# The opening of a planned convolution and max-out kernel: VectorE's tap products read the softmax weights from a PSUM bank, TensorE sums the taps of four tiles, and the opening's list is written anew

## The chip, the cores and the metric

The kernel runs on one core of one Trainium2 chip. The time is device microseconds (us) of one execution of the whole program. The kernel before takes 1434.37 us, the median of three runs (1434.16 to 1434.89).

The core has five engines that run side by side, each through its own list of instructions in order: TensorE (PE in the profile; its weight loads are PEld), VectorE (DVE), ScalarE (ACT), GpSimd (POOL) and SyncE (SP), which here issues the DMAs. SBUF is the working memory; PSUM has eight banks, which TensorE writes.

## The reference, cut to what matters

```python
w = softmax(weight_gen, over the 7 taps)          # [8, 4160, 8 heads, 7 taps]
out = einsum('bshk,bskhg->bshg', w, x_unf)        # x_unf: each token with the 6 before it
x = out.reshape(33280, 192)
h = maximum(maximum(x @ w1, x @ w2), x @ w3)      # 192 -> 768
return h @ w_out                                  # 768 -> 192
```

Everything is fp32. The weights come as float64 (the kernel reads them as pairs of 32-bit words).

## The kernel before

**Tiling.** 33280 tokens are 260 tiles of 128, and 65 chunks of 4 tiles. Chunk 0 is a load of its own; from chunk 1 on two chunks share one load of tokens (tile `xt`, two buffers) and of tap weights (`wt`).

**A chunk's way.** The softmax of the tap weights runs over DVE, POOL and ACT (lines 366 to 405). For each tile a *tap product* (L428) multiplies the tokens with the weights, 7 taps by 192 numbers, into a buffer `r`, and a *sum* on DVE (L440) adds the 7 taps into `acc`. The product runs on POOL, or on DVE for the tiles in `TAPS_ON_VECTOR`. Then the tile is turned, so that features lie on partitions: for chunks 0 and 1 by TensorE (L481, L482) into two PSUM banks, for the others by DVE and 24 ACT moves into `room`. ACT and DVE or POOL split the result into a high and a low part (`xa_hi`, `xa_lo`, `xb`, `xc`).

**The maxima.** max(xw1, xw2, xw3) is taken as xw1 + max(0, x(w2-w1), x(w3-w1)). So `up` multiplies with two differences (high and low parts `wa_hi`, `wa_lo`, `wb_hi`, `wb_lo`) for each of the six blocks j of 128 hidden features, ACT and DVE take the maximum, and split it into `h_hi` and `h_lo`. `down` multiplies those with w_out, and x with `wca` and `wcb`, the product of w1 and w_out, which the opening makes (`compose`, L870). Both have their matmuls at line 922. Each is cut into two half-height rows of 64 partitions, planned as two streams, L and U, that TensorE runs at the same time.

**What sets the order.** Nothing is written in program order. The kernel makes tasks with an engine, an assumed cost, dependencies, a due time and the buffers they hold; `Plan.order` (line 71) plays them through event by event and lets each free engine take the ready task with the earliest due. Two kinds, the TensorE streams L and U, run in the order in which they are added. For chunks 0 and 1 that order is the hand-written list `OPENING` (line 222): loads, softmax, `singles` (float64 words to fp32, lines 638 to 689), `a` and `b` (the differences, on POOL, or on TensorE where `MODE` says L), `turn` (w1 turned for `compose`, L851 and L853), `turn x` (a tile turned), `parts`, `up`, `compose`, `down`. Tables beside it say which engine takes what: `MODE`, `CLAMP_ON_POOL`, `ON_POOL_FIRST`, `LOAD_DUE`, `TAPS_ON_VECTOR`, `SUMS_ON_TENSOR` (empty before).

An engine's own list is then fixed: an instruction that waits holds up all behind it on that engine.

```python
        ("a", 2): ("POOL", "DVE"),     # line 186: difference on POOL, its low part ("rest") on DVE
        ("b", 2): ("L", "DVE"),        # line 189: difference on TensorE, rest on DVE
    SUMS_ON_TENSOR = ()
    TAPS_ON_VECTOR = ((0, 3), (1, 0), (1, 2))   # (chunk, tile)
```

Of the kernel before, what the change touches and what calls it, by code (L numbers as in the profile page):

```python
# [17 lines left out]
P = 128  # L18
# [21 lines left out]
class Plan:  # L40
# [13 lines left out]
    def add(self, engine, cost, emit, deps=(), due=None, holds=(), end=None):  # L54
# [6 lines left out]
        return t  # L61

    def start_by(self):

        for t in reversed(self.tasks):
            latest = [a.by - self.LATENCY - t.end for a in t.after]
            if t.due is not None:
                latest.append(t.due)
            t.by = min(latest, default=1e6)

    def order(self):
# [20 lines left out]
        def start(t, now):  # L92
# [53 lines left out]
def lightconv_maxout_kernel(  # L146
# [44 lines left out]
    CLAMP_ON_POOL = (("a", 1, 0), ("a", 1, 1), ("a", 2, 0), ("a", 2, 1), ("a", 2, 2), ("b", 1), ("d", 0), ("d", 1),)  # L191
    LOAD_DUE = {
        ("s", 0): -46,
        ("a", 0): -61,
        ("b",): -36,
        ("s", 1): -45,
        ("a", 1): -51,
        ("a", 2): -36,
        ("d",): -21,
    }  # L200
# [8 lines left out]
    for c in range(1, NC):  # L209
# [14 lines left out]
        ("load down",), ("softmax", 0), ("softmax", 1), ("singles", 0), ("singles", 1),  # L224
        ("singles", 2), ("singles down",), ("taps", 0), ("taps", 1), ("turn", 0), ("b", 2),
# [6 lines left out]
    )  # L232
# [67 lines left out]
    def vec(n):  # L300
        return 0.062 + 0.00104 * n
# [105 lines left out]

    parts_of, last_product = {}, {}

    def taps(c):  # L410
        s = super_of[c]
        la = (c - supers[s][0]) * TC
        hx, hw, ha = xts[s], wts[s], hold("acc")
        sums = []
        for t in range(TC):
            hr = hold("r")
            eng, cost = ("DVE", vec(D * K)) if (c, t) in TAPS_ON_VECTOR else ("POOL", 2.68)
            on = nc.vector if eng == "DVE" else nc.gpsimd
            by_tensor = (c, t) in SUMS_ON_TENSOR

            def product(t=t, hr=hr, on=on, by_tensor=by_tensor):
# [17 lines left out]
            def total(t=t, hr=hr):  # L439
                pin(nc.vector.tensor_reduce(buf(ha)[:, t], buf(hr), axis=AX.X, op=ALU.add))  # L440

            p = plan.add(
                eng, cost, product, [ready[s], *loads[s][1]], early(c, 3 * t - 17), [hr, hx, hw]
            )
            sums.append(
                (p, hr)
# [43 lines left out]
    def blocks(c, ha, sums):  # L490
# [19 lines left out]
        for q, f in enumerate(range(0, D, 32)):  # L510
            for p in range(0, P, 32):
# [6 lines left out]

                got.append(plan.add("ACT", 0.31, move, [turned], clock[0] - 2 + q, [hv]))
        return [hv], lambda: places()[:2], got  # L520

    def parts(c, hs, places, got):
# [13 lines left out]
            for h in halves  # L536
        ]
        name, cost = ("DVE", vec(CH)) if c < ON_TENSOR else ("POOL", gps(CH))
        eng = nc.vector if c < ON_TENSOR else nc.gpsimd
# [151 lines left out]
    w_hi, w_lo, b_hi, b_lo, one_a, one_b = {}, {}, {}, {}, {}, {}  # L691
    of_bank = {}

    def whole(cost, emit, deps, holds):

        got = plan.add(
            "L", cost, emit, [*deps, made, *u_last()], clock[0], holds, end=cost + 0.25
        )
        clock[0] += cost
        return got  # L700
# [22 lines left out]
    def difference(shape, w, of, deps, holds, on):  # L723
# [3 lines left out]
        if on == "POOL":  # L727
# [8 lines left out]
            )  # L736
            return w, d, holds
        hb = hold("bank")

        def mult():  # L740
# [13 lines left out]
        d = whole(0.1 + n * m * 0.0034, mult, [*deps, made_minus], [hb, *holds])  # L754
        return lambda: buf(hb)[:, : n * m].rearrange("p (i n) -> p i n", i=n), d, [hb]

    def rest(size, to, of, hi, deps, holds, on):

        eng = nc.gpsimd if on == "POOL" else nc.vector
        return plan.add(  # L760
# [4 lines left out]
    def differences_a(jp, first, last):  # L765
# [3 lines left out]
        n = last - first  # L769
        v, d, holds = difference(  # L770
            (n, 2 * P), lambda: buf(hx)[:, first:last],
# [8 lines left out]
        )  # L780
        lo = rest(
            2 * n * P, lambda: place_of(wa_lo), of, lambda: place_of(wa_hi).bitcast(F32), [hi],
            holds, then,
        )
        for i in range(first, last):
            w_hi[jp, i], w_lo[jp, i] = hi, lo

    def differences_b(jp):
        hq = hold("bhi")
        on, then = MODE["b", jp]  # L790
        v, d, holds = difference(
            (NI, P), lambda: b32[:, jp, 1:], lambda: b32[:, jp, 0], [one_b[jp]], [], on
# [3 lines left out]
        )  # L796
        b_lo[jp] = rest(
            2 * P, lambda: wb_lo[:, jp], v, lambda: buf(hq).bitcast(F32), [e], [*holds, hq], then
        )
        for odd, h in enumerate(halves):  # L800
# [285 lines left out]

    def ups(c, j):
        for i in range(NI):
            up(c, j, i)

    def singles_down():
# [6 lines left out]
        "turn x": turn_tokens, "parts": opening_parts,  # L1098
        "a": differences_a, "b": differences_b, "up": ups,
        "turn": turn_weights, "compose": compose, "down": downs,  # L1100
    }
# [54 lines left out]
```

## Time and profile before

| | |
|---|---|
| median of three runs | 1434.37 us |
| the profiled execution | 1434.17 us |
| its span, first to last instruction | 1432.4 us |
| so outside the span | 1.8 us |
| PE busy | 1399.5 us (98%) |
| ACT, POOL, DVE busy | 78%, 77%, 71% |
| mean granted TensorE clock | 0.993 |

The page's numbers are of one execution. PE is busy nearly all the time, but a matmul at half clock is as busy as one at full clock, so the share says little about the opening. What matters is read in stretches, and from the distance between the starts of neighbouring instructions.

### The profile page before, as it was taken

The page shows a single profiled execution, that of the slowest core. Times are in us where ns is not written, and L with a number is a line of the kernel's source. Part 1 is how long each engine was busy: PE and PEld are TensorE (multiplying, and loading weights), DVE is VectorE, ACT ScalarE, POOL GpSimd, SP SyncE. Part 2 cuts the span into 40 slices and gives each one's busy share as a digit, 9 for nine tenths or more (in the row PEclk, how much of TensorE's full clock was granted, in tenths as well). Part 3 has the DMA queues.
Part 4 walks back from the last instruction along what each step waited for, and adds up shares of the span by engine and source line. Part 5 has one row for each costly group of instructions (what it writes and reads, how often), then busy time and mean ns, then how long its engine had stood idle before and what let it go on. Part 6 is the DMA issues. An engine that isn't in the chain of part 4 may idle for free.

```text
span 1432.4 us, 37054 instructions
## 1 busy us (share of the span) xinstructions
PE 1399.5 (98%) x14884; PEld 1341.8 (94%) x14884; DVE 1021.9 (71%) x1394; ACT 1117.7 (78%) x2860; POOL 1105.1 (77%) x609
## 2 busy tenths in 40 slices
PE   3999999999999999999999999999999999999999
PEld 2799999999999999999999999999999999999998
DVE  8877777777677767767776776777687677767543
ACT  4378787888878878887887888888787887888773
POOL 6889978988686987868798786888868688886521
PEclk9799999999999999999999999999999999999999
DMA  7011111111111011111101111110111111110000
GB/s 251 1 57 69 68 57 69 68 65 61 68 69 57 33 60 57 68 68 68 58 23 69 58 68 68 57 66 26 63 63 69 68 57 42 50 58 24 24 23 24
DMA packets 23004, 85.09 MB, mean 59 GB/s; under 512 B 2488, under 2 KB 9144, under 8 KB 18864
## 3 DMA queue, kind: packets, MB, share of 16 engines
q1 hardware_dynamic: 22832, 82.73, 15.7%
q8 instruction: 116, 1.90, 0.5%
q14 instruction: 56, 0.46, 0.1%
HBM read 57.16 MB, written 25.56 MB: 58 GB/s over the span
## 4 chain that ended last, share of the span: by engine, by line
PE 77%; POOL 9%; DVE 8%; issue 3%; ACT 2%; DMA 0%; SPq 0%; DVEq 0%; POOLq 0%
PE bank L922 76%; POOL r L428 6%; DVE acc L440 3%; DVE bank L987 2%; DVE h_lo L998 1%; POOL h_lo L998 1%; POOL xb L549 1%; POOL xa_lo L544 1%; ACT h_hi L991 1%; DVE m L987 1%; ACT room L517 1%; ACT m L979 0%; POOL wt L403 0%; PE bank L870 0%; DVE r L428 0%
## 5 line engine op out<-in xcount | busy, mean ns | idle before, releaser
L428 POOL TENSOR_TENSOR r<-xt,wt 128x1344 f32<-128x1344 f32 x257 | 715.4, 2853 | 22.3 <-DMA xt<-in_x_dram 19.0
L922 PE MATMUL bank<-wo,h_hi 64*128 64x384 f32 x3120 | 660.1, 355 | 0.0
L922 PE MATMUL bank<-wo,h_lo 64*128 64x192 f32 x3120 | 593.5, 249 | 0.9
L922 PE MATMUL bank<-xa_hi,wa_hi 64*128 64x512 f32 x1560 | 507.9, 392 | 0.4 <-ACT wb_hi L805 0.3
L922 PE MATMUL bank<-xa_lo,wa_hi 64*128 64x512 f32 x1560 | 507.2, 391 | 0.0
L922 PE MATMUL bank<-xa_hi,wa_lo 64*128 64x512 f32 x1560 | 502.8, 388 | 0.0
L922 PEld LDWEIGHTS bank<-wo,h_lo 64*128 64x128 f32 x3120 | 482.5, 187 | 8.0 <-DVE h_lo L998 6.2
L517 ACT COPY room<-room 32x128 f32<-32x128 f32 x1512 | 447.9, 296 | 41.7 <-DVE room L506 19.3
L922 PEld LDWEIGHTS bank<-wo,h_hi 64*128 64x128 f32 x3120 | 475.3, 185 | 0.0
L440 DVE TENSOR_REDUCE acc<-r 128x192 f32<-128x1344 f32 x260 | 398.2, 1543 | 18.9 <-POOL r L428 18.5
L998 POOL TENSOR_TENSOR h_lo<-m,h_hi 128x512 fp32r<-128x512 f32 x132 | 174.2, 1320 | 179.9 <-ACT h_hi L991 179.7
L922 PE MATMUL bank<-xc,wb_hi 64*128 64x512 f32 x780 | 295.7, 388 | 0.0
L979 ACT ACTIVATE m<-bank 128x512 f32<-128x512 f32 x390 | 233.9, 600 | 64.8 <-PE bank L922 61.5
L922 PE MATMUL bank<-xb,wb_hi 64*128 64x512 f32 x780 | 280.4, 390 | 0.1
L922 PE MATMUL bank<-xc,wb_lo 64*128 64x512 f32 x780 | 276.5, 388 | 0.0
L922 PEld LDWEIGHTS bank<-xa_lo,wa_hi 64*128 64x128 f32 x1560 | 266.9, 185 | 9.2 <-POOL xa_lo L544 0.4
L922 PEld LDWEIGHTS bank<-xa_hi,wa_hi 64*128 64x128 f32 x1560 | 264.7, 185 | 10.5 <-ACT raw L858 0.8
L922 PEld LDWEIGHTS bank<-xa_hi,wa_lo 64*128 64x128 f32 x1560 | 265.1, 185 | 8.5
L987 DVE TENSOR_TENSOR bank<-bank,m 128x512 f32<-128x512 f32 x258 | 175.6, 694 | 81.7 <-PE bank L922 62.0
L1055 DVE TENSOR_TENSOR o<-bank,ob 128x192 f32<-128x192 f32 x260 | 90.2, 351 | 189.0 <-ACT ob L1048 188.5
L998 DVE TENSOR_TENSOR h_lo<-bank,h_hi 128x512 fp32r<-128x512 f32 x258 | 172.5, 680 | 51.2 <-ACT h_hi L991 49.9
L991 ACT CAST h_hi<-bank 128x512 fp32r<-128x512 f32 x258 | 151.1, 586 | 66.6 <-DVE bank L987 63.3
(92 smaller groups left out, 2046.1 us busy)
## 6 DMA issues: line engine op xcount, KB each, us to landing
xt<-in_x_dram SPq DMA_DIRECT2D x31, 1344.0 KB, 5.6
out_dram<-o SPq DMA_DIRECT2D x64, 384.0 KB, 2.3
wt<-in_weight_gen_dram SPq DMA_DIRECT2D x32, 224.0 KB, 5.9
h_hi<-in_moe_w_dram SPq DMA_DIRECT2D x6, 256.0 KB, 4.4
h_lo<-in_moe_w_dram SPq DMA_DIRECT2D x6, 192.0 KB, 7.8
xt<-in_x_dram SPq DMA_DIRECT2D x1, 960.0 KB, 6.9
raw<-in_moe_w_dram SPq DMA_DIRECT2D x3, 256.0 KB, 6.0
room<-in_moe_w_out_dram SPq DMA_DIRECT2D x2, 384.0 KB, 6.3
```

Of the source, the lines that this page charges most:

```text
L428: on.tensor_tensor(to, buf(hx)[:, la + t : la + t + K].rearrange("p k (h g) -> p k h g", g=G), buf(hw)[:, la + t] .rearrange("p (h k) -> p ...
L440: pin(nc.vector.tensor_reduce(buf(ha)[:, t], buf(hr), axis=AX.X, op=ALU.add))
L517: pin(nc.scalar.copy(to[:, :, p : p + 32], b[p : p + 32, :, f : f + 32]))
L544: eng.tensor_tensor(buf(al), places()[0], buf(ah).bitcast(F32), op=ALU.subtract)
L549: eng.tensor_tensor(buf(b)[halves[low]], places()[1], buf(k)[near].bitcast(F32), op=ALU.subtract)
L922: ins = nc.tensor.matmul(buf(hb)[:, :n], w()[h], v()[h], start=half == 0 and first, stop=half == 1 and last,)
L979: lambda: pin(nc.scalar.activation(buf(hm), buf(hb), AF.Relu)), [made], due,
L987: lambda: pin(nc.vector.tensor_tensor(buf(keep), buf(hb), buf(hm), op=ALU.max)),
L991: "ACT", act(CH), lambda: pin(nc.scalar.copy(buf(hh)[:, j], buf(keep))), [m], due + 1,
L998: eng.tensor_tensor(buf(hl)[:, j], buf(keep), buf(hh)[:, j].bitcast(F32), op=ALU.subtract)
L1055: nc.vector.tensor_tensor(buf(ho)[:, t], buf(hb)[:, :D], buf(hq), op=ALU.add)
```

## The change

- **Where VectorE's product reads.** For a chunk with tiles in `TAPS_ON_VECTOR`, ACT first copies those tiles' softmax weights (56 numbers a partition each) into a PSUM bank, and DVE's product reads them there. POOL's products read `wt` as before.
- **Which tiles.** `TAPS_ON_VECTOR` is (0,1), (0,3), (1,3).
- **TensorE sums taps.** For (0,1), (0,2), (0,3) and (1,3) the product is written with the taps outermost, and `turn x` becomes 14 fp32 matmuls with the identity, 7 for each of two banks, that add up the taps and turn them at once. DVE's sums of these four tiles go, and so do their plain turns.
- **No rest by DVE from SBUF.** `MODE`: the rest of a2 goes to POOL; the b difference made by TensorE is now b0, its rest on DVE from the bank; b2's goes to POOL. (A rest on TensorE can be asked for with `rests`, and idle matmuls with `warm`; the tables use neither.)
- **The list.** All tiles of chunks 0 and 1 are turned before the first `up`, and the `up`s of both chunks follow without a turn between them. Loads have new due times, clamps and the first chunks' low parts of h other engines.
- **The planner.** It assumes doubled costs for L and U in windows after one with little TensorE work, and 0.12 us more for an ACT move that follows another kind of ACT instruction. The second touches the order of all chunks.

```diff
-    SUMS_ON_TENSOR = ()
+    SUMS_ON_TENSOR = ((0, 1), (0, 2), (0, 3), (1, 3),)
-    ON_POOL_FIRST = (0, 1, 5)
-    TAPS_ON_VECTOR = ((0, 3), (1, 0), (1, 2))
+    ON_POOL_FIRST = (2,)
+    TAPS_ON_VECTOR = ((0, 1), (0, 3), (1, 3))
-        ("a", 2): ("POOL", "DVE"),
-        ("b", 0): ("POOL", "POOL"),
+        ("a", 2): ("POOL", "POOL"),
+        ("b", 0): ("L", "DVE"),
-        ("b", 2): ("L", "DVE"),
+        ("b", 2): ("POOL", "POOL"),
...
+        mine = [t for t in range(TC) if (c, t) in TAPS_ON_VECTOR]
+        if mine:
+            hb, n = hold("bank"), len(mine)
+            near = lambda: buf(hb)[:, : n * H * K].rearrange("p (t k) -> p t k", t=n)
+            def bring():
+                for q, t in enumerate(mine):
+                    pin(nc.scalar.copy(near()[:, q], buf(hw)[:, la + t]))
+            brought = plan.add("ACT", n * act(H * K), bring, [ready[s]], early(c, -18), [hb, hw])
...
+            wide = (lambda t=t: near()[:, mine.index(t)]) if t in mine else (lambda t=t: buf(hw)[:, la + t])
-                        buf(hw)[:, la + t]
+                        wide()
...
+            cost, end = t.cost, t.end
+            if t.engine in self.FIXED:
+                k = self.pace(now)
+                cost, end = k * cost, k * end
+            elif t.apart:
+                before = last.get(t.engine)
+                if before is not None and not before.apart and now - busy[t.engine] < 0.05:
+                    cost, end = cost + 0.12, end + 0.12
```

How the order moves, at the three places that matter. First TensorE's list from its start, before (`w1a` and `b32` are the weights being turned or subtracted, `acc` chunk 0's summed taps):

```order
L851 MATMUL bank_256<-ident_58,w1a_66 128x128
L853 MATMUL bank_256<-ident_58,b32_68 128x64 x2
L743 MATMUL bank_266<-b32_68,ident_58 128x256
L749 MATMUL bank_266<-b32_68,minus_67 128x128 x2
L481 MATMUL bank_273<-ident_58,acc_227 128x128
L482 MATMUL bank_275<-ident_58,acc_227 64x128
```

and now (L517 is the sum of taps, `r` the products; L527 and L528 the plain turn, L967 and L969 a turn of weights):

```order
L517 MATMUL bank_213<-ident_58,r_199 128x128 x7
L517 MATMUL bank_214<-ident_58,r_199 64x128 x7
L527 MATMUL bank_213<-ident_58,acc_231 128x128
L528 MATMUL bank_214<-ident_58,acc_231 64x128
L517 MATMUL bank_213<-ident_58,r_208 128x128 x7
L517 MATMUL bank_214<-ident_58,r_208 64x128 x7
L967 MATMUL bank_308<-ident_58,w1a_66 128x128
```

Two tiles of chunk 0 now stand ahead of every turn of weights. Second, TensorE where chunk 1 is turned (into `bank_531` and `bank_533`); before, three of its tiles stood behind five of chunk 0's six blocks of `up`, and the fourth behind the sixth. Here the third tile, and the sixth block after it:

```order
L851 MATMUL bank_539<-ident_58,w1a_66 128x128
L853 MATMUL bank_539<-ident_58,b32_68 128x64 x2
L481 MATMUL bank_531<-ident_58,acc_478 128x128
L482 MATMUL bank_533<-ident_58,acc_478 64x128
L922 MATMUL bank_549<-xa_hi_302,wa_hi_59 128x512
L922 MATMUL bank_549<-xa_lo_316,wa_hi_59 128x512
L922 MATMUL bank_549<-xc_306,wb_hi_61 128x512
```

and now (chunk 1 in `bank_416` and `bank_418`); behind these rows come two more plain turns of chunk 1 and then the first `up` of all:

```order
L527 MATMUL bank_416<-ident_58,acc_406 128x128
L528 MATMUL bank_418<-ident_58,acc_406 64x128
L517 MATMUL bank_416<-ident_58,r_379 128x128 x7
L517 MATMUL bank_418<-ident_58,r_379 64x128 x7
L967 MATMUL bank_450<-ident_58,w1a_66 128x128
L969 MATMUL bank_450<-ident_58,b32_68 128x64 x2
```

The `up`s no longer have chunk 1's turns in their way, and wait for them instead. Third, POOL around its first products of chunk 1, before:

```order
L731 TENSOR_TENSOR wx_346<-wx_346,w1a_66 128x512
L403 TENSOR_TENSOR wt_150<-wt_150,den_354 128x448
L659 TENSOR_SCALAR m_352<-m_352 128x384
L428 TENSOR_TENSOR r_425<-xt_262,wt_150 128x7x192
L998 TENSOR_TENSOR h_lo_461<-m_407,h_hi_434 128x512
```

and now:

```order
L856 TENSOR_TENSOR wa_lo_60<-wx_248,wa_hi_59 128x2x2x128
L472 TENSOR_TENSOR r_377<-xt_263,wt_204 128x7x192
L472 TENSOR_TENSOR r_398<-xt_263,wt_204 128x7x192
L472 TENSOR_TENSOR r_437<-xt_263,wt_204 128x7x192
L794 TENSOR_TENSOR wx_364<-wx_364,w1a_66 128x512
```

Chunk 1's three POOL products now stand in one block, ahead of the last difference of the weights.

More of the change, by code (lines that the diff above doesn't have):

```diff
@@ L31, in __init__ @@
         self.holds, self.after = holds, []
+        self.share, self.apart = 0.5, False
         self.end = cost if end is None else end
@@ L61, in add, with pace, worked @@
         return t
+    def pace(self, now):
+        while (self.window + 1) * self.WINDOW <= now + self.SHIFT:
+            self.slow = self.work.get(self.window, 0.0) < self.ENOUGH * self.WINDOW
+            self.window += 1
+        return 2.0 if self.slow else 1.0
+    def worked(self, now, cost, share):
+        end = now + cost
+        while now < end - 1e-9:
+            w = int((now + self.SHIFT + 1e-6) // self.WINDOW)
+            to = min(end, (w + 1) * self.WINDOW - self.SHIFT)
+            self.work[w] = self.work.get(w, 0.0) + (to - now) * share
+            now = to
     def start_by(self):
@@ L77, in order @@
         taken = set()
+        self.window, self.slow, self.work = -1, True, {}
+        last = {}
         for t in self.tasks:
@@ L442, in taps @@
             p = plan.add(
-                eng, cost, product, [ready[s], *loads[s][1]], early(c, 3 * t - 17), [hr, hx, hw]
+                eng, cost, product, [brought if t in mine else ready[s], *loads[s][1]],
+                early(c, 3 * t - 17), [hr, hx, hb if t in mine else hw],
             )
+            products_of[c, t] = p
             sums.append(
@@ L537, in parts @@
         ]
+        for t in cs:
+            t.apart = True
         name, cost = ("DVE", vec(CH)) if c < ON_TENSOR else ("POOL", gps(CH))
@@ L692, in lightconv_maxout_kernel, with warm, mult @@
     of_bank = {}
+    later = {}
+    def warm(n, *after):
+        hb = hold("bank")
+        what, *which = after
+        deps = {"softmax": ready, "one_a": one_a, "one_b": one_b, "product": products_of}[what]
+        def mult():
+            for _ in range(n):
+                pin(nc.tensor.matmul(buf(hb)[:, :P], minus, ident, start=True, stop=True))
+        whole(0.22 * n, mult, [deps[which[0] if len(which) == 1 else tuple(which)], made_minus], [hb])
     def whole(cost, emit, deps, holds):
@@ L698, in whole @@
         )
+        got.share = 1.0
         clock[0] += cost
@@ L736, in difference, with terms @@
             )
-            return w, d, holds
+            return w, d, holds, lambda: [(ident, w(), slice(0, n))]
         hb = hold("bank")
+        def terms():
+            return [(ident, w(), slice(0, n)), *((minus, of().unsqueeze(1), slice(i, i + 1)) for i in range(n))]
         def mult():
@@ L769, in differences_a @@
         n = last - first
-        v, d, holds = difference(
+        v, d, holds, terms = difference(
             (n, 2 * P), lambda: buf(hx)[:, first:last],
@@ L780, in differences_a, with low, rests @@
         )
[L781 to L784, printed above, removed]
-        for i in range(first, last):
-            w_hi[jp, i], w_lo[jp, i] = hi, lo
+        def low():
+            lo = rest(
+                2 * n * P, lambda: place_of(wa_lo), of, lambda: place_of(wa_hi).bitcast(F32), [hi],
+                [hx] if then == "L" else holds, then, terms,
+            )
+            for i in range(first, last):
+                w_lo[jp, i] = lo
+        for i in range(first, last):
+            w_hi[jp, i] = hi
+        if then == "L":
+            later.setdefault(("a", jp), []).append(low)
+        else:
+            low()
+    def rests(*which):
+        for f in later.pop(which, ()):
+            f()
     def differences_b(jp):
@@ L790, in differences_b @@
         on, then = MODE["b", jp]
[L791 removed]
+        v, d, holds, terms = difference(
             (NI, P), lambda: b32[:, jp, 1:], lambda: b32[:, jp, 0], [one_b[jp]], [], on
@@ L796, in differences_b, with low @@
         )
-        b_lo[jp] = rest(
-            2 * P, lambda: wb_lo[:, jp], v, lambda: buf(hq).bitcast(F32), [e], [*holds, hq], then
-        )
+        def low():
+            b_lo[jp] = rest(
+                2 * P, lambda: wb_lo[:, jp], v, lambda: buf(hq).bitcast(F32), [e],
+                [hq] if then == "L" else [*holds, hq], then, terms,
+            )
+        if then == "L":
+            later["b", jp] = [low]
+        else:
+            low()
         for odd, h in enumerate(halves):
@@ L1087, in ups @@
     def ups(c, j):
+        rests("a", j // 2)
+        rests("b", j // 2)
         for i in range(NI):
@@ L1098, in lightconv_maxout_kernel @@
         "turn x": turn_tokens, "parts": opening_parts,
-        "a": differences_a, "b": differences_b, "up": ups,
-        "turn": turn_weights, "compose": compose, "down": downs,
+        "rests": rests, "a": differences_a, "b": differences_b, "up": ups,
+        "warm": warm, "turn": turn_weights, "compose": compose, "down": downs,
     }
```

69 lines of the change are left out of this document (52 added, 17 removed), and 9 rows, old and new, of the table OPENING.

## The prediction

> **What bounds the kernel now.** I read first the busy time by stretches, cut where TensorE (PE) changes its work. Columns: stretch and length, busy us (and instructions) of PE, PEld, DVE, ACT and POOL, the granted clock, DMA share, GB/s.
>
> ```profile
> 0.00:23.95 23.95, 0.45 (x1) 0.18 (x1) 18.86 (x38) 8.09 (x18) 16.38 (x18) 1.00 0.95 307
> 23.95:32.95 9.00, 7.61 (x28) 5.21 (x29) 8.56 (x16) 6.24 (x16) 5.96 (x10) 1.00 0.49 183
> 32.95:49.42 16.47, 16.40 (x90) 13.55 (x90) 15.71 (x15) 8.89 (x22) 12.77 (x8) 1.00 0.00 1
> 49.42:69.05 19.63, 16.18 (x53) 12.56 (x53) 15.96 (x23) 7.13 (x15) 17.88 (x10) 0.57 0.00 0
> 69.05:1432.40 1363.35, 1358.84 (x14713) 1310.25 (x14712) 962.81 (x1306) 1087.30 (x2791) 1052.14 (x565) 1.00 0.15 56
> ```
>
> In the last stretch PE is busy 1358.84 of 1363.35 us, and ACT, next, 1087.30. It holds all of chunk 1's `up`s and everything after; only an earlier start of it moves the end much. So the opening, 69.05 us, is where the change can win: there PE idles 28 us, and for part of the rest its clock is halved, as the distance between starts shows (start, duration, engine, line):
>
> ```profile
> 25.43 1.06 PE L749 MATMUL bank<-b,minus 128*128 128x128 f32 x4
> 26.29 0.42 PE L481 MATMUL bank<-ident,acc 128*128 128x128 f32 x1
> ...
> 33.52 0.62 PE L922 MATMUL bank<-xa_lo,wa_hi 64*128 64x512 f32 x1
> 33.94 0.62 PE L922 MATMUL bank<-xc,wb_hi 64*128 64x512 f32 x1
> ...
> 40.26 0.39 PE L922 MATMUL bank<-xa_lo,wa_hi 64*128 64x512 f32 x1
> 40.49 0.39 PE L922 MATMUL bank<-xc,wb_hi 64*128 64x512 f32 x1
> ...
> 62.74 6.39 PE L870 MATMUL bank<-wo,raw 128*128 128x192 f32 x24
> 69.05 0.49 PE L922 MATMUL bank<-xa_hi,wa_hi 64*128 64x512 f32 x1
> ```
>
> The same matmul starts 0.42 us after its neighbour at 33.5 and 0.23 us at 40.3: half clock, then full, though the clock column has 1.00 in both (it has no record that early). From 49.42 to 69.05 the column itself has 0.57. Two fp32 matmuls of L749 are four records, 0.86 us to the next row: **0.215 us a record of 128 columns at half clock**, 0.11 at full. Then the waits of PE in the first 90 us:
>
> ```profile
> PE bank L853 <- DVE b L683: 17.2, 1, 17.2
> PE bank L481 <- DVE acc L440: 2.7, 2, 1.5
> ```
>
> PE starts late on DVE, and halfway through chunk 0's `up`s it stops for chunk 1's summed taps, cools down, and runs L870 and `up`s at half clock. DVE is the engine behind both:
>
> ```profile
> 7.25 0.41 DVE L683 SCALAR_TENSOR_TENSOR wx<-h_hi,bank 128x256 uint32<-128x256 uint32 x1
> 7.58 0.42 DVE L674 SCALAR_TENSOR_TENSOR bank<-h_hi,bank 128x256 uint32<-128x256 uint32 x1
> ...
> 14.13 2.56 DVE L428 TENSOR_TENSOR r<-xt,wt 128x1344 f32<-128x1344 f32 x1 [1.17 <-POOL wt L403]
> 16.72 1.55 DVE L440 TENSOR_REDUCE acc<-r 128x192 f32<-128x1344 f32 x1
> ...
> 20.57 1.02 DVE L659 TENSOR_SCALAR bank<-bank 128x384 f32<-128x384 f32 x2
> 21.50 1.02 DVE L665 TENSOR_SCALAR bank<-bank 128x384 uint32<-128x384 uint32 x2
> ...
> 37.52 2.91 DVE L762 TENSOR_TENSOR wa_lo<-wx,wa_hi 128x512 fp32r<-128x512 f32 x1
> 40.53 0.69 DVE L987 TENSOR_TENSOR m<-bank,m 128x512 f32<-128x512 f32 x1
> 41.14 6.39 DVE L428 TENSOR_TENSOR r<-xt,wt 128x1344 f32<-128x1344 f32 x2
> ```
>
> ```profile
> 13.52 0.58 POOL L403 TENSOR_TENSOR wt<-wt,den 128x224 f32<-128x224 f32 x1
> 14.17 9.91 POOL L428 TENSOR_TENSOR r<-xt,wt 128x1344 f32<-128x1344 f32 x3
> ...
> 37.32 2.69 POOL L428 TENSOR_TENSOR r<-xt,wt 128x1344 f32<-128x1344 f32 x1
> 41.96 2.98 POOL L998 TENSOR_TENSOR h_lo<-m,h_hi 128x512 fp32r<-128x512 f32 x1 [1.95 <-ACT h_hi L991]
> ...
> 54.80 1.28 POOL L998 TENSOR_TENSOR h_lo<-m,h_hi 128x512 fp32r<-128x512 f32 x1
> ```
>
> Where DVE takes both inputs from SBUF, it and POOL shut each other out. DVE's L762 lasts 2.91 us beside POOL's product, though L987 of the same size, with one input in PSUM, leaves room for the next after 0.61. POOL's L998 takes 2.98 beside DVE's products and 1.28 alone; its first product beside DVE's takes 4.9 of the 9.91.
>
> **The change, part by part.** *DVE from a bank.* No row has this product. By L987 (0.61 for 512) and L440 (1.55 for 1344, and the next may start a little earlier) it would be 1.5 us; by the SBUF product 2.56. I take 1.5, since one input in PSUM and a dense output make it like L987, and keep 2.56 as the other end. The Trainium skill ("VectorE: DVE Perf Modes", the errata section) gives (N+151)/0.96 ns for an fp32 tensor_tensor, an estimate of 1.56 us here even from SBUF; the row has 2.56, so the row decides, and by the page's figure this term would shrink by the same 0.06 us a product.
>
> *The first products* come after wt's softmax. Its load was SP's seventh and is now its fourth, and DVE's maximum has five instructions ahead of it, not fifteen:
>
> ```profile
> 0.74 2.76 SPq L598 DMA_DIRECT2D h_hi<-in_moe_w_dram  x6
> 3.54 0.43 SPq L332 DMA_DIRECT2D wt<-in_weight_gen_dram  x1
> ...
> 24.11 0.35 SPq L337 DMA_DIRECT2D xt<-in_x_dram  x1
> ```
>
> ```profile
> 5.82 0.40 ACT L654 ACTIVATE bank<-h_hi 128x256 f32<-128x256 f32 x1 [1.30 <-DMA h_hi<-in_moe_w_dram]
> ...
> 10.10 0.39 ACT L385 ACTIVATE wt<-wt 128x224 f32<-128x224 f32 x1
> ```
>
> Maximum at 6.1 (loads are issued 0.47 apart, and the third one's words were there at 5.8), subtract to 7.1, exp 7.6, sum 8.4 behind four instructions of 0.33, reciprocal 9.3, multiply (0.58, behind a rest of 0.7) 10.4, ACT's copies of 56 numbers 10.8 (0.1 to 0.4 by ACT's shorter rows). DVE's products: 10.8 to 13.8, where they stood at 14.13. POOL's first stands beside them unblocked: 11.1 to 13.8.
>
> *DVE then.* One sum (1.5) instead of four (6.0) for chunk 0. From 13.8 to chunk 1's product stand that sum, 15 instructions of 256 (0.33), 12 of 384 (0.46), two weight sums (0.53) and a reciprocal (0.5): 1.5 + 5.0 + 5.5 + 1.1 + 0.5 = 13.6, so 27.4. L732's last w1a, for which the third turn of weights waits, is at 24.6.
>
> *Chunk 1's tokens* need chunk 0's buffer. POOL's last product there ends at 13.8 + a clamp and a rest (1.1) + 2.65 = 17.5, where it was 24.08; the load is then issued 6.6 us earlier, but behind 7.0 MB of other loads, which in this trace last to about 24.5.
>
> ```profile
> GB/s 0 23 287 336 244 340 372 431 424 355 329 234 246 241 247 253 370 378 373 375 413 410 413 281 14 237 409 387 382 192 8 0 0 0 0 0 0 0 0 0
> ...
> xt<-in_x_dram SPq DMA_DIRECT2D x1, 1344.0 KB, 5.7
> ```
>
> That is the rate of each of the first 40 us, and the load's 5.7 us on an empty queue. At 380 GB/s it needs 3.6 behind the others: landed at 28.2 (between 17.5 + 5.7 = 23.2 and the 29.8 of before). POOL's three products follow, at 2.65 each (2.69 in the row, 2.5 in the three): 28.2 + 8 = 36.2, after its rests, which end at 27.3. DVE, busy with two sums, chunk 0's low parts and a clamp, is free at 36.5; the last sum ends at 38.0, its turn (two records) at 38.5. **So the first `up` starts at 38.5**, 5.5 us later than before, but with nothing more to wait for.
>
> *TensorE's sums.* 28 records a tile, four tiles: 112 x 0.215 = 24 us at half clock, 12 at full, less eight plain turns (1.7). The first two lie where PE was idle (0.45 busy up to 23.95): 12.4 to 20.8. (0,2) waits behind the third turn, 24.6, and ends at 30.7 at the latest; turns and the b0 difference to 32.8; (1,3) to 36 at full clock. All end before 38, so I cost them at nothing. POOL's displaced rests and differences (0.7 to 1.3 each) end at 39.8; the block that needs the last one starts at 40.8.
>
> *From the first `up`.* Chunk 0's six blocks are 108 half-height matmuls, two at a time: 54 x 0.23 = 12.4. L870's 24 records have 192 columns: 24 x 0.16 = 3.9 at full clock. Start with one stream and a window of half clock, as at 33 to 40: 3.4 us at half, 1.7 lost. The work that ended at 69.05 then ends at 38.5 + 12.4 + 3.9 + 1.7 = **56.5**: 12.55 us gained.
>
> *All other chunks.* The planner's dearer ACT moves shift ACT's list there; PE's streams keep their work. I take 0, and 2.5 us either way.
>
> The sum: 1434.17 (the profiled execution; the median is 0.2 above) - 12.55 = **1421.6**.
>
> **Rivals.** *(a) The bank product takes 2.56.* 1.1 more for each of three products, all in DVE's row before the last sum: 3.3 us later, 1424.9. For it: no row shows another product. Against: L987.
>
> *(b) PE at half clock.* If turns don't warm PE, the sums of (0,2) and (1,3) run at half clock: 32.8 + 6 + turns, the first `up` at 41.7 with two windows at half: 41.7 + 16.3 + 3.4 = 61.4, and the time is 1426.5. In the second stretch PE was busy 7.61 of 9.00 us, much of it turns, and L922 at 33.5 still ran at half clock. The Trainium skill ("TensorE: Matmul & The Clock Gate", Part 4) says that transposes don't count as PE work for the gate; the row agrees, and by it this rival gains.
>
> *(c) Given back later.* Chunk 2 becomes due 12.5 us earlier. Its path through `room` took from 73.83 to 91.9:
>
> ```profile
> 73.83 0.97 DVE L506 STREAM_TRANSPOSE room<-acc 128x768 f32<-128x768 f32 x1
> ...
> 90.60 1.30 POOL L549 TENSOR_TENSOR xb<-room,xc 64x512 fp32r<-64x512 f32 x1
> ```
>
> By POOL's new row chunk 2's four products and three low parts of w_out (about 1 each) follow 39.8 and end at 53.3; a sum and the path make 53.3 + 1.5 + 18.1 = 72.9. It is needed at 56.5 + 12.4 + 8.8 = 77.7 (a chunk's `down`s are 8.8: 1363 less 64 x 12.4, over 65). If it came no earlier than before, PE would wait all of 12.5 us: no difference, 1434.
>
> *(d) Slower.* ACT's reordered moves make each later chunk's low parts or banks late, and PE's in-order row waits. 64 chunks: from 0.2 us a chunk the gain is gone; at 0.3 it costs 19 us, 1441. Against: ACT has 276 us free in the last stretch, PE waits 4.5 us in all of it.
>
> That it doesn't do what it says can't be: the copies and L517 stand in the lists.
>
> **How the numbers follow.** Forecast 0.62 (1418 to 1425), (a) 0.11, (b) 0.14, (c) 0.08, (d) 0.05. The range 1416 to 1429 takes in the forecast, (a), (b) and the loads' early end, and leaves out (c), (d) and a little. 0.2% (2.9 us) is about what a measurement of this kernel can tell from no change: faster 0.87, same 0.07, slower 0.06.
>
> **What would show it.** In the changed profile: DVE's L472 at 1.5 us, not 2.6, and POOL's products at 2.65 beside it; the tokens of chunk 1 landed at 28; the first L1038 at 38.5, 0.23 us apart after one window at most; the 24 records of L986 in 3.9 us; chunk 1's own `up`s from about 56; the rest of the span 1363 us. The prediction is wrong if L1038 starts after 45, if PE waits again among the `up`s, or if the rest is longer than 1366.

## The result, and the profile after

The changed kernel takes 1419.1 us, the median of four runs (1417.27 to 1421.38), against 1434.26 us before (four runs too): a ratio of 0.9896, 95% interval 0.9878 to 0.9914, or 15.2 us. The forecast was 1421.6, range 1416 to 1429. The profiled execution took 1417.27 us, its span 1415.5: 16.9 us less than the profiled execution of before. In all that follows one execution, of e4, took 4768 us; it is left out of that kernel's ratio.

By stretches, cut at the first `up`, at `compose` and behind it (columns as before):

```profile
0.00:38.64 38.64, 21.33 (x144) 18.25 (x145) 33.99 (x65) 21.33 (x54) 29.63 (x35) 1.00 0.69 234
38.64:52.85 14.21, 14.21 (x109) 12.76 (x109) 13.40 (x20) 8.80 (x16) 14.21 (x9) 1.00 0.00 1
52.85:56.95 4.10, 4.10 (x26) 3.88 (x25) 4.10 (x7) 1.56 (x4) 2.22 (x3) 1.00 0.73 260
56.95:1415.50 1358.55, 1354.32 (x14713) 1317.39 (x14712) 968.43 (x1304) 1092.60 (x2790) 1046.28 (x562) 1.00 0.15 55
```

The work that ended at 69.05 ends at 56.95. Behind that point both kernels have the same 14713 matmul records, but they take 1358.55 us where they took 1363.35. So of the 16.9 us **12.1 come from the opening and 4.8 from all that follows**. The six blocks of `up` between the two points are not all chunk 0's any more: the new list has five of chunk 0 and one of chunk 1 ahead of `compose`, which is as much work. TensorE's instructions in the opening:

```profile
12.23 5.75 PE L517 MATMUL bank<-ident,r 128*128 128x128 f32 x28 [12.23 <-DVE r L472]
...
18.18 3.40 PE L517 MATMUL bank<-ident,r 128*128 128x128 f32 x28
...
24.88 3.50 PE L517 MATMUL bank<-ident,r 128*128 128x128 f32 x28
...
38.27 0.33 PE L527 MATMUL bank<-ident,acc 128*128 128x128 f32 x1 [1.09 <-DVE acc L484]
38.44 0.27 PE L528 MATMUL bank<-ident,acc 128*64 128x128 f32 x1
38.64 0.49 PE L1038 MATMUL bank<-xa_hi,wa_hi 64*128 64x512 f32 x1
...
40.15 0.50 PE L1038 MATMUL bank<-xa_hi,wa_hi 64*128 64x512 f32 x1
...
52.85 4.17 PE L986 MATMUL bank<-wo,raw 128*128 128x192 f32 x24
56.95 0.49 PE L1038 MATMUL bank<-xa_hi,wa_hi 64*128 64x512 f32 x1
```

The first 28 records take 5.75 us, nearly all at half clock; the next 28, from 18.18, take 3.40, at full clock. From there on no row is stretched again, so the `up`s of this execution never run at half. The turn ahead of the first `up` waits 1.09 us for DVE's last sum; the second stream's first `up` is at 40.15. DVE's and POOL's products:

```profile
10.53 3.02 DVE L472 TENSOR_TENSOR r<-xt,bank 128x1344 f32<-128x1344 f32 x2 [0.58 <-ACT bank L455]
...
27.95 1.55 DVE L472 TENSOR_TENSOR r<-xt,bank 128x1344 f32<-128x1344 f32 x1
...
36.68 1.54 DVE L484 TENSOR_REDUCE acc<-r 128x192 f32<-128x1344 f32 x1
```

```profile
10.65 2.67 POOL L472 TENSOR_TENSOR r<-xt,wt 128x1344 f32<-128x1344 f32 x1
...
28.09 7.73 POOL L472 TENSOR_TENSOR r<-xt,wt 128x1344 f32<-128x1344 f32 x3 [0.56 <-DMA xt<-in_x_dram]
```

DVE's product lasts 1.55 us, and POOL's runs beside it undisturbed, 2.67. Chunk 1's tokens are there at 28: DVE's product of them starts at 27.95, POOL's at 28.09.

### The profile page after: what moved, and what is told of

Same layout as the page of the kernel before. It is cut to its first block, busy times and chain, and to the rows that moved or that the text cites. A ratio compares the mean times of both kernels' runs of the same rounds, so it can differ in the third digit from the quotient of the medians.

```text
span 1415.5 us, 37236 instructions
## 1 busy us (share of the span) xinstructions
PE 1394.0 (98%) x14988; PEld 1352.3 (96%) x14988; DVE 1019.9 (72%) x1393; ACT 1124.3 (79%) x2863; POOL 1092.3 (77%) x606
## 5 line engine op out<-in xcount | busy, mean ns | idle before, releaser
L1038 PE MATMUL bank<-wo,h_hi 64*128 64x384 f32 x3120 | 669.9, 356 | 0.0
L1038 PE MATMUL bank<-wo,h_lo 64*128 64x192 f32 x3120 | 597.1, 248 | 0.7
L1038 PEld LDWEIGHTS bank<-wo,h_lo 64*128 64x128 f32 x3120 | 486.2, 187 | 5.6 <-DVE h_lo L1114 5.6
L563 ACT COPY room<-room 32x128 f32<-32x128 f32 x1512 | 448.3, 297 | 43.6 <-DVE room L552 20.1
L1038 PEld LDWEIGHTS bank<-wo,h_hi 64*128 64x128 f32 x3120 | 478.4, 185 | 0.0
L1038 PE MATMUL bank<-xa_hi,wa_hi 64*128 64x512 f32 x1560 | 470.4, 389 | 0.0
L1038 PE MATMUL bank<-xa_lo,wa_hi 64*128 64x512 f32 x1560 | 469.0, 388 | 0.0
L1038 PE MATMUL bank<-xa_hi,wa_lo 64*128 64x512 f32 x1560 | 467.0, 387 | 0.0
L1095 ACT ACTIVATE m<-bank 128x512 f32<-128x512 f32 x390 | 233.9, 600 | 106.1 <-PE bank L1038 101.0
L1038 PE MATMUL bank<-xc,wb_hi 64*128 64x512 f32 x780 | 280.4, 386 | 0.0
L1038 PE MATMUL bank<-xb,wb_hi 64*128 64x512 f32 x780 | 277.6, 387 | 0.0
L1038 PEld LDWEIGHTS bank<-xa_lo,wa_hi 64*128 64x128 f32 x1560 | 250.5, 184 | 6.7
L1038 PEld LDWEIGHTS bank<-xa_hi,wa_lo 64*128 64x128 f32 x1560 | 250.3, 184 | 6.4
L1038 PE MATMUL bank<-xc,wb_lo 64*128 64x512 f32 x780 | 256.0, 386 | 0.0
L1038 PEld LDWEIGHTS bank<-xa_hi,wa_hi 64*128 64x128 f32 x1560 | 249.4, 184 | 6.8 <-issue 0.4
L1038 PE MATMUL bank<-wca,xa_hi 64*128 64x384 f32 x520 | 184.1, 355 | 0.0
```

The costliest lines, as they stand in the source:

```text
L563: pin(nc.scalar.copy(to[:, :, p : p + 32], b[p : p + 32, :, f : f + 32]))
L1038: ins = nc.tensor.matmul(buf(hb)[:, :n], w()[h], v()[h], start=half == 0 and first, stop=half == 1 and last,)
L1095: lambda: pin(nc.scalar.activation(buf(hm), buf(hb), AF.Relu)), [made], due,
```

## The experiments

One table for all. The columns are the median of a kernel's runs, and, of its one profiled execution, the start of the first `up`, the start of the work behind `compose`, and the time from there to the end of the span (the *rest*).

| kernel | median us | first `up` | behind `compose` | rest |
|---|---|---|---|---|
| before | 1434.26 | 32.95 | 69.05 | 1363.35 |
| changed | 1419.1 | 38.64 | 56.95 | 1358.55 |
| e1_no_apart | 1412.18 | 38.72 | 58.64 | 1352.46 |
| e2_apart_only | 1428.45 | 32.56 | 70.83 | 1358.97 |
| e3_weights_from_sbuf | 1421.21 | 42.38 | 60.67 | 1358.63 |
| e4_no_sums_on_tensor | 1433.98 | 41.27 | 69.36 | 1361.34 |
| e5_changed_again | 1419.94 | 38.51 | 58.42 | 1358.58 |
| e6_fill_pe_idle | 1415.42 | 41.27 | 59.56 | 1354.84 |
| e7_up_before_last_turn | 1414.34 | 38.21 | 58.40 | 1354.60 |
| e8_three_products_more | 1424.12 | 40.03 | 58.34 | 1361.96 |
| e9_planner_of_before | 1412.58 | 39.95 | 58.27 | 1352.33 |
| e10_rest_on_vector | 1415.77 | 39.92 | 59.86 | 1355.34 |
| e11_bank_alone | 1428.44 | 33.08 | 70.32 | 1364.08 |
| e12_bank_alone_again | 1435.99 | 33.08 | 70.35 | 1364.05 |

### Where the 4.8 us behind the opening come from: e1, e2, e9

```diff
-                    cost, end = cost + 0.12, end + 0.12
+                    cost, end = cost + 0.0, end + 0.0
```

> The changed kernel with the 0.12 us that the planner adds for an ACT move after another kind of ACT instruction set to 0; the opening stays as it is. In the changed kernel the work after compose took 1358.55 us where 1363.35 were foreseen, and four chunks of the steady part took 83.98 us where they had taken 84.24. Theory A (the planner's 0.12 made that gain): the steady part goes back to about 84.24 us for four chunks, 0.065 a chunk over some 60 chunks, so the time is 4 us longer, 1423. Theory B (the new opening leaves the steady part in a better order, whatever the 0.12): 83.98 stays, and the time stays at 1419. The first up starts at 38.6 by both.

The second kernel has the twelve lines of the planner that add the 0.12, and the two that mark the moves, in the kernel before:

> The kernel before with nothing new but the planner's 0.12 us for an ACT move after another kind of ACT instruction. Theory A: the steady part goes from 84.24 to about 83.98 us for four chunks, and the time from 1434.3 to 1430.3. Theory B: 84.24 stays, and the time stays at 1434.3. The opening up to 69 us changes little by both.

The third is e1 with

```diff
-        return 2.0 if self.slow else 1.0
+        return 1.0
```

> The changed kernel with the whole planner of before: the 0.12 us at 0 and no doubled costs for TensorE. Without the 0.12 alone it took 1412.2 us, and four steady chunks took 83.50. Theory A (the opening decides into which steady order the planner falls, and the doubled costs do nothing for the time): 83.50 us for four chunks, 1412. Theory B (the doubled costs brought the better order): 84.24 as before the change, so 1412 + 0.185 x 60 = 1423.

ACT's moves of finished tiles, 193 of them over 48 chunks, tell the length of the steady part (count, min/median/max ns, first and last start). Before:

```profile
L1048 ACT COPY ob<-bank x193: 298/319/337, 298.6 to 1309.8; 128x192 f32<-128x192 f32 x193
```

Before with the 0.12 (e2):

```profile
L1060 ACT COPY ob<-bank x193: 298/320/323, 298.7 to 1306.4; 128x192 f32<-128x192 f32 x193
```

Changed:

```profile
L1164 ACT COPY ob<-bank x193: 297/319/322, 284.3 to 1292.0; 128x192 f32<-128x192 f32 x193
```

Changed without the 0.12 (e1):

```profile
L1164 ACT COPY ob<-bank x193: 299/320/328, 286.0 to 1287.9; 128x192 f32<-128x192 f32 x193
```

48 chunks take 1011.2 us before; 1007.7 with the 0.12, in the old opening and in the new one; and 1001.9 with the new opening and without the 0.12. Four chunks are 84.27, 83.98 and 83.49 (e9 has 83.49 too). **Both of e1's theories fall**: the time went down 7 us, not up or nowhere. The planner's greedy choice settles into an order that repeats every four chunks. With the 0.12 it settled at 83.98 from the old opening and from the new; without it, the old opening leads to 84.27 and the new one to 83.49. The other kernels keep close to these three lengths, by the same moves: e3, e4 and e8, with the 0.12, have 83.97 to 83.98; e6, e7 and e10, without it, 83.49 to 83.50; e11, the old opening without it, 84.32. e9 shows that the doubled costs play no part in the time: 1412.58, ratio 0.9855 (0.9842 to 0.9868), beside e1's 0.9851 (0.9837 to 0.9864). e2's 1428.45, 0.9963 (0.995 to 0.9977), has the gain that its theory A gave the 0.12 in the old opening, and 1.9 us more; but its six runs spread with the mean granted clock, from 1425.2 at 0.999 to 1431.6 at 0.992, so the lengths of four chunks say more here than the medians.

Where the time lies can be seen in part from the waits of PE's weight loads over the same 48 chunks (total us, times, longest). Before, and changed:

```profile
PEld bank L922 <- DVE h_lo L998: 6.2, 24, 0.4
PEld bank L922 <- POOL xb L549: 1.0, 5, 0.4
```

```profile
PEld bank L1038 <- DVE h_lo L1114: 4.5, 12, 0.4
PEld bank L1038 <- SPq L1044: 1.2, 8, 0.2
```

In the changed kernel a weight load waits 0.4 us for a low part of h once in four chunks; in e1 the view has no row at all. Those 5.7 us fit the 5.8 between e1 and the changed kernel. Between before and changed the rows explain 1.5 of 3.5; where the rest lies isn't shown. PE's busy time doesn't set such waits apart. This is e1 behind `compose` (columns as before):

```profile
58.64:1411.10 1352.46, 1348.65 (x14713) 1296.93 (x14712) 963.15 (x1304) 1079.73 (x2790) 1046.19 (x562) 1.00 0.16 55
```

The same 14713 records stand in 1352.46 us, which is less than PE's busy time before, 1358.84. So that busy time held waiting too.

The 0.12 itself is close to what the trace shows. ACT in the changed kernel:

```profile
60.52 0.60 ACT L1095 ACTIVATE m<-bank 128x512 f32<-128x512 f32 x1
61.14 1.22 ACT L563 COPY room<-room 32x128 f32<-32x128 f32 x4
62.38 0.59 ACT L1107 CAST h_hi<-bank 128x512 fp32r<-128x512 f32 x1
62.87 0.61 ACT L1095 ACTIVATE m<-bank 128x512 f32<-128x512 f32 x1
```

Behind L1107 the next activation starts after 0.49 us; behind L1095 a move starts only after 0.62, 0.13 later. The truer assumption leads to a better order from one opening and to a worse one from the other.

### The bank and the layout of the product: e3, e4, e11

e3 leaves the tables alone and takes the copies away:

```diff
-        mine = [t for t in range(TC) if (c, t) in TAPS_ON_VECTOR]
+        mine = []
```

> The changed kernel, but VectorE's three tap products read the softmax weights from SBUF, and ACT's copies go. Theory A (the bank shortens the product and lets POOL work beside it): the products last 2.56 us instead of 1.55, POOL's products beside them stretch to about 5, the last sum of chunk 1 ends 1.5 to 3.3 us later, the first up starts at 40 to 42, and the time is 1421 to 1422.5. Theory B (the products are hidden anyway, chunk 1's tokens set the end): the first up stays at 38.6 and the time at 1419.

e4 takes TensorE's sums away:

```diff
-    SUMS_ON_TENSOR = ((0, 1), (0, 2), (0, 3), (1, 3),)
+    SUMS_ON_TENSOR = ()
```

> The changed kernel, but all eight tiles of chunks 0 and 1 are summed on DVE and turned plainly; TensorE sums no taps. DVE has four more sums of 1.54 us. Theory A (DVE is what the first up waits for, and the taps' sums keep TensorE's clock up): the first up starts about 6 us later, at 44.5, and runs two windows at half clock, 3.4 us lost; 1419 + 6 + 3.4 = 1428. Theory B (DVE sets the end, but plain turns keep the clock up as well): 1425. Theory C (DVE had room, the tokens of chunk 1 set the end): 1419 to 1421.

e11 puts the copies and the reading from the bank, and nothing else, into the kernel before:

> The kernel before with nothing new but the bank: VectorE's products of (0,3), (1,0) and (1,2) read the weights that ACT has copied to PSUM. Theory A (the products of 2.56 and 6.39 for two become 1.5 and 3.0, and chunk 1's turns, for which PE stops among chunk 0's ups, come some 3 us earlier): 1431 to 1432. Theory B (without TensorE's sums and the new list DVE and POOL give it back, or the bank is missed elsewhere): 1434 or more.

The products of e3 (DVE, then POOL):

```profile
10.23 5.90 DVE L472 TENSOR_TENSOR r<-xt,wt 128x1344 f32<-128x1344 f32 x2
...
30.16 3.08 DVE L472 TENSOR_TENSOR r<-xt,wt 128x1344 f32<-128x1344 f32 x1
```

```profile
10.83 3.94 POOL L472 TENSOR_TENSOR r<-xt,wt 128x1344 f32<-128x1344 f32 x1
```

and of e4 and e11 on DVE, and e11's on POOL:

```profile
10.59 5.01 DVE L472 TENSOR_TENSOR r<-xt,bank 128x1344 f32<-128x1344 f32 x2 [0.58 <-ACT bank L455]
...
29.29 2.58 DVE L472 TENSOR_TENSOR r<-xt,bank 128x1344 f32<-128x1344 f32 x1
```

```profile
14.61 2.58 DVE L439 TENSOR_TENSOR r<-xt,bank 128x1344 f32<-128x1344 f32 x1 [1.41 <-ACT bank L422]
```

```profile
14.41 7.63 POOL L439 TENSOR_TENSOR r<-xt,wt 128x1344 f32<-128x1344 f32 x3
```

Two things that the change joins come apart here. The **bank** takes the lock away, by which DVE and POOL shut each other out: POOL's three products of chunk 0 take 7.63 in e11, where they took 9.91 before. The **length** of DVE's product comes from how it writes: a tile that DVE sums is written with the taps innermost, 7 numbers apart, and takes 2.58 even from the bank; a tile that TensorE sums is written densely and takes 1.55. In e3 the output is dense too, and yet the products take 2.95 each and 3.08. There the lock is the likely reason: two of 1.55 and one of POOL's 2.67 make 5.77, about the 5.90 that DVE's two take. No run has a dense product from SBUF with POOL idle; the nearest row is e10's L856 below, dense and from SBUF, at 0.68 us for 512. The Trainium skill ("SBUF — State Buffer", "Who interferes with whom") says that a DVE instruction with two SBUF inputs contends with a GpSimd instruction that reads SBUF; the trace agrees, 3.94 beside such a product and 2.67 beside one from the bank.

e3 went as its theory A said: the first `up` is 3.7 us later, the work behind `compose` too, the rest unchanged at 1358.63, and the median 1421.21, 0.9918 (0.9904 to 0.9931). The profiled executions lie 3.9 us apart (1421.12 and 1417.27), the medians only 2.1, for half of the changed kernel's runs are at 1420 to 1422 with a lower clock (see e5).

e4 went A's way and further, 15 us where A had 9: 1433.98, 0.9999 (0.999 to 1.0008). Without TensorE's sums the new opening is worth nothing. Four more sums and three longer products delay everything else on DVE. Here is what PE waits for between 30 and 75 us:

```profile
PE bank L967 <- DVE w1a L732: 6.5, 1, 6.5
PE bank L1038 <- SPq L1044: 1.2, 1, 1.2
PE bank L527 <- DVE acc L484: 0.8, 1, 0.8
PE bank L1038 <- DVE wb_lo L856: 0.8, 1, 0.8
PE bank L969 <- DVE b L732: 0.6, 1, 0.6
PE bank L1038 <- POOL wa_lo L856: 0.4, 1, 0.4
```

The first `up` starts at 41.27, only 2.6 us later, but 6.5 us of waiting stand ahead of it and 2.4 us (the rows of L1038) among the `up`s. TensorE, which did little but turn up to then, is at half clock behind the first `up`s. Columns of the stretch as above:

```profile
45.00:50.00 5.00, 4.55 (x17) 2.89 (x16) 3.67 (x8) 2.57 (x5) 5.00 (x3) 0.50 0.00 0
```

`compose` starts at 63.75 where it stood at 52.85, and the rest is 2.8 longer.

e11's twelve runs fall into two groups, eight at 1427.7 to 1429.1 with mean clocks of 0.997 to 0.999, and four at 1436 with 0.990 to 0.994; the profile is of one of the four. Its theory A missed: chunk 0's product is no shorter (2.58 where 2.56 stood), and chunk 1's two take 2.81 and 2.62, less than the 6.39 of before but not the 3.0 of theory A. e12 is e11 once more. Its expectation counts nine short runs and three long ones; eight and four is right.

> The kernel of e11_bank_alone again, for a profile of one of its short executions: nine of its twelve took 1428 at mean clocks of 0.997 to 0.999, three 1436 at 0.990 to 0.994, and the profile fell on one of the three. Theory A (the bank frees POOL, so that chunk 1's turns come earlier in every run, and the clock makes the 8 us between the two kinds of run: 0.007 of 1430 us is 20 us of half clock, 10 lost): in a short execution the third of chunk 1's turns stands at 51 to 54, as in the long one or little earlier, with two windows of half clock or fewer between 20 and 70 us, and the work after compose starts at 62 to 63.5 instead of 70.3; the steady part has 84.24 us for four chunks in both. Theory B (something in the steady part differs between the two kinds): the work after compose starts at 68 or later, and the steady part is shorter.

The profile was again of a long execution, its first `up` at 33.08 and the work behind `compose` at 70.35, and of its eight runs two took 1428 and six 1435 to 1437; the ratio is 1.0 (0.9978 to 1.0021). In all twenty runs of this kernel, ten short and ten long, the short ones have the higher clock. By an estimate from these clocks, 0.006 of 1434 us is 8.6 us of full-speed work, as much as lies between the groups; but no short execution was profiled. So what the bank alone is worth, and what parts the two groups, stays open.

### The clock: e5, e6

e5 is the changed kernel as it is.

> The changed kernel as it is, for the spread of its runs: four had 1417.3, 1417.9, 1420.3 and 1421.4 at mean granted clocks of 0.999, 0.999, 0.997 and 0.996. Theory A (windows of half clock in the opening, which fall differently from run to run, make the spread): each run at 0.999 takes 1417 to 1418, each at 0.996 or 0.997 takes 3 to 4 us more, since 0.003 of 1416 us is 8.5 us at half speed, 4.2 lost if PE is busy. Theory B (the spread is something else): times and clocks don't go together.

Its stretches (columns as above, the clock third from the end) and TensorE's third group of sums:

```profile
0.00:38.51 38.51, 22.20 (x144) 19.02 (x144) 33.88 (x65) 21.37 (x53) 30.02 (x35) 0.96 0.69 234
38.51:54.32 15.81, 15.81 (x110) 13.99 (x109) 13.40 (x20) 8.68 (x16) 14.65 (x9) 0.89 0.03 6
```

```profile
24.89 5.11 PE L517 MATMUL bank<-ident,r 128*128 128x128 f32 x28
```

The same instructions, started at nearly the same times up to there, had a stretch of half clock among the third sums (5.11 us where 3.50 stood) and one among the `up`s (15.81 us for 14.21). The first cost nothing, the second 1.6, and the execution took 1.5 more. Of the eight runs of the changed kernel the three at 0.999 took 1417.3 to 1418.3, three at 0.997 1418.8 to 1421.1, two at 0.996 1421.4 and 1421.9. Times and clocks go together, as theory A says, if not by its 3 to 4 us each time. The Trainium skill ("TensorE: Matmul & The Clock Gate", Part 1) says that the clock is set by windows of 3413 ns that run free of the kernel's start; the trace agrees as far as one program had half clock at different places in two executions.

e6 fills PE's waits, with e1's planner. The new task is in the opening's list twice:

```diff
-        ("turn x", 0, 3), ("turn", 4), ("turn", 5), ("turn", 3), ("turn x", 0, 2),
+        ("turn x", 0, 3), ("turn", 4), ("turn", 5), ("warm", 10, "one_b", 0), ("turn", 3), ("turn x", 0, 2),
-        ("turn", 2), ("turn x", 1, 1), ("parts", 0), ("b", 2), ("rests", "b", 2), ("turn x", 1, 2),
+        ("turn", 2), ("turn x", 1, 1), ("parts", 0), ("b", 2), ("rests", "b", 2), ("warm", 5, "one_b", 0), ("turn x", 1, 2),
```

> The changed kernel with the planner's 0.12 us at 0 (1412.2 us as it stands) and 15 idle fp32 matmuls on TensorE: 10 behind the second turn of weights, where PE waited 2.3 us, and 5 ahead of chunk 1's last turn, where it waited 1.1. Theory A (too little matmul work in a window makes the next one half as fast; the profile of the kernel without them had half clock at 26.3 to 29.7 and 40.0 to 43.4): the clock stays full from the first sums on, 0.999 in all runs, and the time is 1409 to 1410. Theory B (the windows don't hang on such gaps): clock and time as without them, 1411 to 1413, or 1 us more where the filling itself is in the way.

The clock did as A said: no stretch of half clock from 20 us to 65 in the profiled execution, and 0.998 or 0.999 in all four runs, where e1 had 0.997 and 0.998. The time did not: 1415.42, 3 us more than e1. The planner, given two more tasks, ordered DVE's and POOL's work anew; the first `up` came at 41.27, and PE waited for low parts of the next chunks' tokens (the row is of 58 to 140 us; e1 has none there). The rest is 2.4 us longer than e1's:

```profile
PE bank L1038 <- POOL xa_lo L593: 0.6, 2, 0.4
```

### The order of turns and ups, and the work on DVE and POOL: e7, e8, e10

e7 and e10 are made from e1, e8 from the changed kernel.

```diff
-        ("turn", 2), ("turn x", 1, 1), ("parts", 0), ("b", 2), ("rests", "b", 2), ("turn x", 1, 2),
-        ("up", 0, 0), ("up", 0, 3), ("up", 0, 4), ("parts", 1), ("rests", "a", 2), ("up", 0, 1),
+        ("turn", 2), ("turn x", 1, 1), ("parts", 0), ("b", 2), ("rests", "b", 2),
+        ("up", 0, 0), ("turn x", 1, 2), ("up", 0, 3), ("up", 0, 4), ("parts", 1), ("rests", "a", 2), ("up", 0, 1),
```

> The changed kernel with the planner's 0.12 us at 0 (1412.2 us), and chunk 0's first block of up moved ahead of chunk 1's last turn in the opening's list. Theory A (PE's last wait for DVE's sum is on the path): the first up starts 1.6 us earlier, at 37.1, and the time falls by 1.1 to 1.6 us. Theory B (a turn between the ups makes both streams of PE meet, which costs about as much as the wait, 1.3 us): the time stays within 0.5 us of 1412.2.

TensorE in e7:

```profile
38.21 0.49 PE L1038 MATMUL bank<-xa_hi,wa_hi 64*128 64x512 f32 x1
...
41.99 0.33 PE L527 MATMUL bank<-ident,acc 128*128 128x128 f32 x1
42.16 0.27 PE L528 MATMUL bank<-ident,acc 128*64 128x128 f32 x1
42.36 0.49 PE L1038 MATMUL bank<-xa_hi,wa_hi 64*128 64x512 f32 x1
```

One block of `up`s stands alone for 3.8 us, and with the turn for 4.15, where six blocks in a row take 14.2 (2.4 each). A turn among the `up`s makes both streams end and start again, and that costs more than the 1.1 us of waiting that it fills: with its `up`s at full clock the work behind `compose` starts at 58.40, where the changed kernel, with its own at full clock, had 56.95. With a rest 2.1 us longer than e1's the median is 1414.34, 2.2 us above e1: theory B's cause, but four times the 0.5 us that it allowed.

```diff
-    TAPS_ON_VECTOR = ((0, 1), (0, 3), (1, 3))
+    TAPS_ON_VECTOR = ((0, 1), (0, 3))
```

> The changed kernel, but chunk 1 has no product on DVE: POOL makes all four, after the tokens land at 28.1. Theory A (landed tokens, POOL's products and the last sum set the first up, as the prediction's sum has it): POOL's fourth product ends 2.6 us later, the first up starts at 41.2 to 41.4, and the time is 2.6 us longer than the changed kernel's. Theory B (DVE's other work sets it): the first up starts at 37 to 38.6, and the time is the same or 1.5 us shorter, since DVE has one product of 1.55 us less.

```profile
27.79 10.24 POOL L472 TENSOR_TENSOR r<-xt,wt 128x1344 f32<-128x1344 f32 x4
```

Theory A's direction with half its size: the first `up` stands at 40.03, 1.4 us later and not 2.6. In the changed kernel POOL's third product ends at 35.82, but the last sum starts at 36.68 only, for DVE is busy until then; here the fourth product ends at 38.03, 2.2 later, and 0.9 of that was covered. So DVE's row set the first `up`, with POOL's close behind. The profiled executions, both at 0.999, lie 4.8 us apart (the median is 1424.12; 0.9932, 0.9919 to 0.9944), since the rest is 3.4 longer as well; by ACT's moves of finished tiles that lies in the third and fourth chunk, 23.2 and 22.1 us where 20.8 and 21.3 stood.

```diff
-        ("a", 2): ("POOL", "POOL"),
+        ("a", 2): ("POOL", "DVE"),
```

> The changed kernel with the planner's 0.12 us at 0 (1412.2 us), and the rest of a2 back on VectorE, from SBUF, as before the change. Theory A (the rest locks POOL out, as DVE's 2.91 us beside POOL's product did before): DVE's L856 of 512 lasts 1.3 to 2.9 us, it stands among the sums or just behind them, and the time is 1 to 3 us longer, 1413 to 1415. Theory B (it finds room behind the last sum): the first up stays at 38.7 and the time within 0.7 us of 1412.2.

```profile
26.11 0.68 DVE L856 TENSOR_TENSOR wa_lo<-wx,wa_hi 128x512 fp32r<-128x512 f32 x1
```

Here POOL had nothing to do at that moment, and this low part took 0.68, not the 2.91 that the same operation took before. The first `up` came 1.2 us later than in e1, but it does in e9 as well, whose DVE and POOL lists are e1's up to 60 us: in both the first product of chunk 1, for which its tokens must be there, starts later on DVE (29.37 and 28.89, where e1 has 28.04). The time behind the opening is 2.9 longer. The 3.6 us between the medians (1415.77) are more than A's range, and most of them lie behind the opening, not where A looked.

## Why the prediction was right, step by step

- **The product from the bank.** 1.5 forecast, 1.55 measured, and POOL free beside it. The reason named two things, an input in PSUM and a dense output; e4 and e11 show that the length hangs on the second and the lock on the first. Rival (a)'s 2.56 is what the bank gives without the dense output, so of the two reasons against it only the dense output held. The Trainium skill's 1.56 ("VectorE: DVE Perf Modes", the errata section) was set aside for the row of 2.56, whose output was strided; the dense product's 1.55 agrees with it, though from the bank. By that figure the 1.5 of the forecast would be 1.56.
- **DVE's row, the tokens, POOL's products, the first `up`.** First products 10.53 (10.8 forecast), tokens 28.09 (28.2), POOL's three done at 35.82 (36.2), last sum at 38.2 (38.0), first `up` 38.64 (38.5). e3 shows the price of DVE's row, 3.7 us in the opening where rival (a) had 3.3, though with POOL's lock in it too.
- **TensorE's sums at nothing.** They ended at 21.6, 28.4 and 36.3 (20.8, 30.7 at the latest and 36 forecast) and held nothing up. What they are worth was never a term: e4 puts it at 15 us, through DVE's sums, the dense products and the clock together; their shares aren't parted.
- **From the first `up` to 56.95.** Forecast 12.4 + 3.9 + 1.7 = 18.0, measured 14.2 + 4.1 = 18.3, and no clock loss. Two errors met, and that they cancel is luck: the 1.7 for a window of half clock wasn't due in this execution (e5 lost 1.6 there), and 12.4 for the `up`s left out that the second stream starts 1.5 us behind the first (40.15 in this trace), so that one of them runs alone at either end. The prediction calls the six blocks chunk 0's; one of them is chunk 1's, and the sum is the same. Before, this path took 36.1 us. Of the 17.8 us gained there, up to 8.4 are the clock, by an estimate from the row up to 69.05: 19.63 us at 0.57, so 0.43 x 19.63.
- **All other chunks: the step that failed.** "I take 0, and 2.5 us either way" was 4.8. The streams kept their work, but the planner fell into another repeating order, of 83.98 us for four chunks instead of 84.27; over 48 chunks that is 3.5 us, and the other 1.3 lie in the chunks around them. Its sign was chance: the same 0.12 costs 5.8 us there against what the new opening would have had without it (e1). The reading behind the 0 was that PE, busy 1358.84 of 1363.35 us, leaves 4.5 to be had; e1's rest is 10.9 us shorter, and 10.2 of that is PE's busy time. So busy time holds waiting as well; the short waits of weight loads are the likely part of it.
- **Rivals.** (b) holds in part: half clock among the `up`s comes and goes between executions, and goes with the step from runs of 1417 to runs of 1421. (c) didn't happen, but e6, e7, e8 and e10 show that it is near: each spends 2.1 to 3.4 us more behind the opening. (d) turned its sign.

**The version that beats both kernels** is e1, the change without the 0.12: 1412.18 us, a ratio of 0.9851 to the kernel before.

## What to carry to other kernels

A product that another engine sums can be written in the order that suits the writer: here that took 1 us of 2.6 from it, and moving one input to PSUM let two engines work at once. Where a greedy planner sets the order of a long steady part, a change of its costs or of its start can move the whole into another repeating order; read the length of some cycles of it from the trace, and try the cost at zero too. Before weighing a shift of work, take the run's granted clock: between two executions of the changed kernel it went with up to 4.6 us.

## What the runs showed of the hardware that was not expected

- DVE's product of 1344 from a PSUM bank: 1.55 us with a dense output, 2.58 with one of 7 numbers' step. POOL's product beside either takes about what it takes alone, 2.5 to 2.7.
- A move of 32 partitions on ACT (L563) starts 0.02 us behind the end of the instruction before it, where L1095 behind L1107 starts 0.1 ahead of that end.
- The changed kernel, run again, had two stretches of half clock behind its first sums (5.11 us where 3.50 stood, 15.81 where 14.21 stood) or none, and the kernel with the bank alone split into 1428 and 1436 us. The cause of the latter wasn't found.
- With the same 14713 matmul records behind the opening, PE was busy 1358.84 us before and 1348.65 in e1: the busy time of PE is not its work alone.
